# One load for 24 rows of wo, one load for wq, and multiplications of zeros ahead of the output projection

## The chip, the cores and the metric

One core of a Trainium2 chip runs the whole program. The metric is the device time of one execution in microseconds (us), smaller is better. "Span" is the time from the first to the last instruction in a profiled execution; it is about 1.9 us shorter than the device time.

The load queue is served by 16 DMA engines. A load of a 128-partition tile becomes 128 runs of contiguous bytes (packets in the trace), one for each partition, eight on each engine. PE is TensorE, DVE is VectorE, ACT is ScalarE, SP is SyncE, which issues nearly all loads here, in program order.

## The reference

A gate `g` mixes two branches of one token `x` of 1,024 numbers. Branch A is grouped attention over a cache of 65,536 positions with 4 groups of 8 query heads; branch B is a small gated feed-forward with a sequence of length 1.

```python
g = sigmoid((x * gate_w).sum(-1, keepdims=True))
q = (x @ wq)                                  # 32 heads of 128
p = softmax(einsum(q, k_cache) * 128 ** -0.5)
a = (p @ v_cache).reshape(1, 1, 4096) @ wo    # wo: 4096 x 1024, 8 MB
b = (z1 * (w_sp * layernorm(z2) + b_sp)) @ w_out
return g * a + (1 - g) * b
```

K and V are 64 MB each, wq and wo 8 MB each, and w_in and w_out 7 and 3.5 MB: 162.0 MB in all (decimal), each byte read once. The rest is small.

## The kernel before

All large loads go into one buffer `kv` of 5 slots. A slot is 32,768 bytes on each of 128 partitions (4 MB), and holds one tile of K or of V (each of the four groups has four of each). A load into a slot can be issued only when the last reader of that slot is done, and SP issues in order.

```python
kv = big.tile([P, NKV * CT * P], BF16, name="kv")          # NKV = 5 slots

def load(src, shape, at):                                   # at: slot, may be a fraction
    ...
    ins = nc.sync.dma_start(out=v, in_=src)
...
win = load(win_view, (KC, F), 3)
wq_t = [load(wq_view[:, i * KH:(i + 1) * KH, :], (KH, HD), 1 - i) for i in range(2)]
...
for g in range(1, G):
    for h in range(2):
        kn = load_kv(A_k_cache, g, 2 * h, 1 - h, 2)         # two K tiles in one load
        for i in ((0, 1), (1, 0))[h]:
            k_tile(g, 2 * h + i, kn[i])                     # DVE transposes, PE scores
        ...
        vn = load_kv(A_v_cache, g - 1, 2 * h, 3, 2)         # two V tiles in one load
        v_tile(g - 1, 2 * h, vn[0])
        if h == 1:
            stats(g)                                        # softmax of group g
        v_tile(g - 1, 2 * h + 1, vn[1])
    head_out(g - 1)                                         # this group's part of oa
for j, n, at in ((0, 2, 1), (2, 1, 3), (3, 1, 4)):          # the last group's V
    ...
keep_busy(4)
head_out(G - 1)
keep_busy(4)
```

The end of the kernel multiplies the attention output `oa` by wo, one loaded piece of rows at a time. `project` does four 128x256 matmuls for a row, on four column groups of the array. ("Row" means one of the 32 rows of wo that each partition holds, 2,048 bytes; a piece of 24 rows is one run of 49,152 bytes on every partition.) `keep_busy(n)` is n matmuls of 128x512 on a weight tile that is mostly zeros; nothing reads what they make.

```python
WO_SPLIT = ((16,), (8, 4, 2, 1, 1))
WO_BUSY = {16: 4, 8: 2, 4: 1, 2: 1, 1: 0}
for at, split in enumerate(WO_SPLIT):
    for n in split:
        t = load(wo_view[:, c0:c0 + n, :], (n, D), at + c0 % (OC // 2) * D / (CT * P))
        project(t, n, oa, c0, last=(c0 + n == OC))
        keep_busy(WO_BUSY[n])
        c0 += n
```

Of the kernel before, what the change touches and what calls it, by code (L numbers as in the profile page):

```python
# [15 lines left out]
P = 128  # L16
CT = 128
NKV = 5
B = 32
NB = P // B  # L20
VC = 4
CC = CT // VC
ZN = 448
HN = 512
WO_SPLIT = ((16,), (8, 4, 2, 1, 1))
WO_BUSY = {16: 4, 8: 2, 4: 1, 2: 1, 1: 0}


@with_exitstack
def kernel(  # L30
# [17 lines left out]
    _, _, D = A_x.shape  # L48
    _, G, S, DH = A_k_cache.shape
    HD = A_wq.shape[1]  # L50
# [4 lines left out]
    KC = D // P  # L55
    FC = FH // P
    OC = HD // P
    QD = P // H
    NT = S // (P * CT)
    HH = HN // DH  # L60
    NHB = HD // (NB * HN)
# [1 line left out]
    SCALE = float(DH) ** -0.5  # L63
    assert NB * VC * REP == P and G * B == P and B == REP * QD and DH == P and D % P == 0
    assert S % (P * CT) == 0 and F == 2 * NB * ZN and ZN == B * FC and HD == NHB * NB * HN
    assert NHB * NB == 2 * G and CC * B == 2 * HN and sum(map(sum, WO_SPLIT)) == OC

    const = ctx.enter_context(tc.tile_pool(name="const", bufs=1))
    wk = ctx.enter_context(tc.tile_pool(name="wk", bufs=2))
# [10 lines left out]
    def same_weights(ins):  # L80
        held.add(ins.ins.name)
# [91 lines left out]
    def load(src, shape, at):  # L173
        n = 1
        for s in shape:
            n *= s
        v = kv[:, int(at * CT * P):int(at * CT * P) + n]
        if len(shape) == 2:
            v = v.rearrange("p (a b) -> p a b", b=shape[1])
        ins = nc.sync.dma_start(out=v, in_=src)  # L180
        if not first_load:
            first_load.append(ins.ins.name)
        return v

    def load_kv(src, g, j, at, n=1):
        h, i = divmod(j, 2)
        rows = src[0, g, 2 * h * CT * P:2 * (h + 1) * CT * P, :].rearrange(
            "(p c) d -> p (c d)", c=2 * CT)
        v = load(rows[:, i * CT * DH:(i + n) * CT * DH], (n * CT * DH,), at)
        return [v[:, i * CT * DH:(i + 1) * CT * DH] for i in range(n)]  # L190
# [9 lines left out]
    KH = KC // 2  # L200
# [1 line left out]
    win = load(win_view, (KC, F), 3)  # L202
    win_t = [win[:, i * KH:(i + 1) * KH, :] for i in range(2)]
    wq_view = A_wq.rearrange("(p c) n -> p c n", c=KC)
    wq_t = [load(wq_view[:, i * KH:(i + 1) * KH, :], (KH, HD), 1 - i) for i in range(2)]


    row = const.tile([P, P], FP32, name="row")
# [147 lines left out]
    for k in range(NHB):  # L356
# [3 lines left out]
                                                                   j=B, e=2),  # L360
# [20 lines left out]
    def build_w(g):  # L381
        for v in range(VC):
            nc.vector.tensor_tensor(
                out=wt[g % 2][:, v, :, :, v, :],
                in0=qs[:, g].unsqueeze(2).to_broadcast([P, BP, NB, REP]),
                in1=own_n[:].unsqueeze(1).unsqueeze(3).to_broadcast([P, BP, NB, REP]),
                op=ALU.mult)

    oa = const.tile([P, OC], BF16, name="oa")
# [3 lines left out]
    def k_tile(g, j, kn):  # L393
        kb = kn.bitcast(I32)
        n = CC * DH // 2
        s_ps = pss.tile([P, 2 * HN], FP32, name="s_ps", tag="s")
        for v in range(VC):
            nc.vector.transpose(out=kb[:, v * n:(v + 1) * n], in_=kb[:, v * n:(v + 1) * n])  # L398
            while late:
                nc.vector.reduce_max(**late.pop())  # L400
            kx = kn[:, v * CC * DH:(v + 1) * CC * DH].rearrange(
                "p (c h k e) -> p h e c k", h=2, k=B, e=2)
            for b in range(BP):
                for k in range(2):
                    ins = nc.tensor.matmul(  # L405
                        s_ps[:, k * HN:(k + 1) * HN],
                        lhsT=wt[g % 2][:, v, b].rearrange("p a v h -> p (a v h)"),
                        rhs=kx[:, b // 2, b % 2, k * CC // 2:(k + 1) * CC // 2, :],
                        start=(v == 0 and b == 0), stop=(v == VC - 1 and b == BP - 1),
                        skip_group_check=True)  # L410
                    if k > 0:
                        same_weights(ins)
        if g not in mxs:
            mxs[g] = wk.tile([P, NT], FP32, name="mx")
        sct[g, j] = scp.tile([P, CC * B], BF16, name="sc")
        nc.scalar.copy(out=sct[g, j][:], in_=s_ps[:])  # L416
        late.append(dict(out=mxs[g][:, j:j + 1], in_=sct[g, j][:], axis=AX.X))
# [26 lines left out]
    def v_tile(g, j, vt):  # L444
        if j == 0:
            o_ps[g] = pso.tile([P, 2, VC * DH], FP32, name="o_ps")
        vx = vt.rearrange("p (v c d) -> p c v d", v=VC, d=DH)
        for u in range(CC // 2):
            hs = slice(u % 2 * P // 2, (u % 2 + 1) * P // 2)
            for e in range(2):  # L450
                ins = nc.tensor.matmul(  # L451
                    o_ps[g][hs, e, :],
                    lhsT=ptt[g, j][:, 2 * u:2 * u + 2, :].rearrange("p c x -> p (c x)"),
                    rhs=vx[:, 2 * u + e], start=(j == 0 and u < 2),
                    stop=(j == NT - 1 and u >= CC // 2 - 2), skip_group_check=True)
                if e > 0:
                    same_weights(ins)
# [28 lines left out]
    def keep_busy(n):  # L486
        ps = pss.tile([P, 2 * HN], FP32, name="busy_ps", tag="s")
        w = wt[G % 2][:].rearrange("p v b t u h -> p (v b t u h)")
        for i in range(n):
            ins = nc.tensor.matmul(ps[:, :HN], lhsT=w[:, :P], rhs=w[:, :HN], start=True,  # L490
                                   stop=True, skip_group_check=True)
            if i > 0:
                same_weights(ins)
# [4 lines left out]
    def project(w, n, vec, c0, first=False, last=False):  # L498
        for c in range(n):
            for t in range(NB):  # L500
                nc.tensor.matmul(  # L501
                    out_ps[t * B:(t + 1) * B, :],
                    lhsT=vec[:, c0 + c:c0 + c + 1].to_broadcast([P, B]),
                    rhs=w[:, c, t * NO:(t + 1) * NO],
                    start=(first and c == 0), stop=(last and c == n - 1),
                    skip_group_check=True)


    build_w(0)
    for j in range(NT):  # L510
        k_tile(0, j, load_kv(A_k_cache, 0, j, (2, 1, 0, 3)[j])[0])
        if j == 1:
            build_w(1)
    project(load(B_w_out.rearrange("(p c) n -> p c n", c=FC), (FC, D), 4), FC, uT, 0, first=True)
    stats(0)
    for g in range(1, G):
        for h in range(2):
            kn = load_kv(A_k_cache, g, 2 * h, 1 - h, 2)
            for i in ((0, 1), (1, 0))[h]:
                k_tile(g, 2 * h + i, kn[i])  # L520
            if h == 0 and g + 1 < G:
                build_w(g + 1)
            vn = load_kv(A_v_cache, g - 1, 2 * h, 3, 2)
            v_tile(g - 1, 2 * h, vn[0])
            if h == 1:
                stats(g)
            v_tile(g - 1, 2 * h + 1, vn[1])
        head_out(g - 1)
    for j, n, at in ((0, 2, 1), (2, 1, 3), (3, 1, 4)):
        for i, vt in enumerate(load_kv(A_v_cache, G - 1, j, at, n)):  # L530
            v_tile(G - 1, j + i, vt)
    keep_busy(4)
    head_out(G - 1)
    keep_busy(4)


    wo_view = A_wo.rearrange("(p c) n -> p c n", c=OC)
    c0 = 0
    for at, split in enumerate(WO_SPLIT):
        for n in split:  # L540
            t = load(wo_view[:, c0:c0 + n, :], (n, D), at + c0 % (OC // 2) * D / (CT * P))
            project(t, n, oa, c0, last=(c0 + n == OC))
            keep_busy(WO_BUSY[n])
            c0 += n
    out_sb = const.tile([P, NO], BF16, name="out_sb")
    out_rows = out.rearrange("o t (q n) -> (o t q) n", n=NO)
    nc.scalar.copy(out=out_sb[:], in_=out_ps[:])  # L547
# [5 lines left out]
    last = {}  # L553
# [37 lines left out]
```

## Time and profile before

| | before |
|---|---|
| device time, median | 382.93 us (3 runs), 382.97 (6 runs beside the changed kernel) |
| load queue's share of the span | 98.8% |
| PE, DVE, ACT busy | 61%, 57%, 10% |
| first load byte to last load byte | 1.0 to 378.4 us |

First the page of the kernel before: the span, the busy time of each engine, PE and DMA in 40 equal slices (tenths), the rate in GB/s per slice, the load queue (packets, MB, share of 16 engines), and the chain of waits by engine and by line.

```profile
span 381.0 us, 2602 instructions
PE 231.0 (61%) x1388; PEld 56.0 (15%) x802; DVE 218.5 (57%) x211; ACT 39.6 (10%) x55; POOL 4.4 (1%) x10
...
DMA  9999999999999999999999999999999999999995
GB/s 385 437 433 423 415 434 440 437 482 430 394 413 440 440 442 433 427 440 440 433 435 440 433 440 433 428 414 420 433 433 442 427 427 434 440 408 433 437 411 234
...
q1 hardware_dynamic: 4180, 162.01, 98.8%
...
DMA 58%; DVE 18%; PE 18%; issue 3%; ACT 2%; SPq 1%; DVEq 0%; ACTq 0%
DMA kv<-in_A_k_cache_dram 43%; PE s_ps L405 14%; DVE kv L398 12%; DMA kv<-in_A_wo_dram 9%; DMA kv<-in_A_v_cache_dram 7%; PE o_ps L451 3%; DVE pt L441 2%; DVE mx L400 2%; DVE o_sb L465 1%; ACT sc L416 1%; ACT sc L438 1%; SPq L180 1%; DVE row
```

The DMA row has no slice under 9 but the last. That is the reading on which everything rests: loads never pause. The chain of waits seems to say otherwise, with 18% each for DVE and PE. It follows one thread of who released whom, and while that thread passes through a DVE or PE instruction the DMA row still shows a full queue.

Figures come from the packet records of the trace, which no view prints. (A record has no engine's number; an engine is followed by matching the start of a packet with the end of the one before.) A run of 65,536 bytes takes one engine 2.421 us (median), which is 27.1 GB/s, or 433 for sixteen. And from first to last load, engines are without a packet for 1.9 us on average, 1.1 of them at the very end, when they finish one after another.

Second, SP's timeline of the kernel before: start, duration, engine, line, operation and what is loaded, how many. A line merges loads whose issue has only waits between.

```profile
1.66 41.59 SPq L180 DMA_DIRECT2D kv<-in_A_k_cache_dram  x4
...
95.18 0.33 SPq L180 DMA_DIRECT2D kv<-in_A_v_cache_dram  x1
118.50 0.33 SPq L180 DMA_DIRECT2D kv<-in_A_k_cache_dram  x1
...
333.56 13.33 SPq L180 DMA_DIRECT2D kv<-in_A_wo_dram  x6
```

The first wo load is issued at 333.56. By the packet records, the first engine finished the last V load ahead of it at 356.4, about 23 us later. That distance between an issue and the moment the queue would run out is the queue's lead.

Third, the end of the kernel before (timeline, weight loads left out; in brackets the idle time before and what ended it).

```profile
369.61 3.54 PE L501 MATMUL out_ps<-kv,oa 128*32 128x256 bf16 x64 [0.43 <-DVE oa L483]
373.09 1.04 PE L490 MATMUL busy_ps<-wt 128*128 128x512 bf16 x4
374.06 1.06 PE L501 MATMUL out_ps<-kv,oa 128*32 128x256 bf16 x32
...
378.96 0.29 PE L501 MATMUL out_ps<-kv,oa 128*32 128x256 bf16 x4 [0.36 <-DMA kv<-in_A_wo_dram]
379.30 0.37 ACT L547 CAST out_sb<-out_ps 128x256 bf16<-128x256 f32 x1 [44.80 <-PE out_ps L501]
```

The 64 matmuls for 16 rows take 3.54 us, 55 ns each; the 32 for the next 8 rows take 1.06, 33 ns each. The difference is PE's clock. The view by windows (us, then busy time and number for PE, weight loads, DVE, ACT, POOL, then the granted clock as a share of full speed, DMA share, GB/s) shows it:

```profile
366.10:369.50 3.40, 1.38 (x6) 0.23 (x3) 2.80 (x6) 0.00 (x0) 0.00 (x0) 1.00 0.94 400
369.50:372.90 3.40, 3.29 (x64) 2.35 (x64) 0.06 (x1) 0.00 (x0) 0.00 (x0) 0.51 0.99 417
```

PE was busy 1.38 of 3.40 us, 41%, and for the next window it got half the clock (0.51). All that costs nothing before: the last four matmuls still wait for the last row to land. (The last two columns count a run in the window in which it begins, so they jump by the length of a run; by the packet records the engines were busy all through both windows.)

### The profile page before, as it was taken

To read this page: it belongs to the slowest core of one execution; us is meant where nothing else is said; L and a number is where in the kernel's file an instruction comes from. 1 tells how busy PE (TensorE), PEld (TensorE's weight loads), DVE (VectorE), ACT (ScalarE), POOL (GpSimd) and SP (SyncE) were. 2 spreads that over 40 slices of the span, in tenths; PEclk is the share of its full clock that TensorE was granted. 3 is DMA by queue.
4 is the path that set the end of the run, shared out by engine and by line. 5 is a ranking of instruction groups with operands and counts; after the bars stand their busy time and mean duration, and the time that the engine had idled before them with its cause. 6 is when DMAs were issued, how large, how long until landed. Compare 5 with 4: busy or idle time off the path is not lost.

```text
span 381.0 us, 2602 instructions
## 1 busy us (share of the span) xinstructions
PE 231.0 (61%) x1388; PEld 56.0 (15%) x802; DVE 218.5 (57%) x211; ACT 39.6 (10%) x55; POOL 4.4 (1%) x10
## 2 busy tenths in 40 slices
PE   0064357677057934695488538872978197938376
PEld 0011011112011200121011101120111011212023
DVE  4143478996678406966976059669770398460040
ACT  1001001111601100114011001050101010410000
POOL 4000000000000000000000000000000000000000
PEclk9996659999759885999598959896789688969689
DMA  9999999999999999999999999999999999999995
GB/s 385 437 433 423 415 434 440 437 482 430 394 413 440 440 442 433 427 440 440 433 435 440 433 440 433 428 414 420 433 433 442 427 427 434 440 408 433 437 411 234
DMA packets 4231, 162.17 MB, mean 426 GB/s; under 512 B 504, under 2 KB 508, under 8 KB 892
## 3 DMA queue, kind: packets, MB, share of 16 engines
q1 hardware_dynamic: 4180, 162.01, 98.8%
q8 instruction: 8, 0.13, 0.1%
q14 instruction: 3, 0.02, 0.0%
q10 hardware_dynamic: 40, 0.01, 0.0%
HBM read 162.01 MB, written 0.00 MB: 425 GB/s over the span
## 4 chain that ended last, share of the span: by engine, by line
DMA 58%; DVE 18%; PE 18%; issue 3%; ACT 2%; SPq 1%; DVEq 0%; ACTq 0%
DMA kv<-in_A_k_cache_dram 43%; PE s_ps L405 14%; DVE kv L398 12%; DMA kv<-in_A_wo_dram 9%; DMA kv<-in_A_v_cache_dram 7%; PE o_ps L451 3%; DVE pt L441 2%; DVE mx L400 2%; DVE o_sb L465 1%; ACT sc L416 1%; ACT sc L438 1%; SPq L180 1%; DVE rowt L461 1%; PE om_ps L471 0%; DVE osum L481 0%
## 5 line engine op out<-in xcount | busy, mean ns | idle before, releaser
L405 PE MATMUL s_ps<-kv,wt 128*128 128x512 bf16 x512 | 139.7, 430 | 85.0 <-DVE kv L398 84.9
L398 DVE STREAM_TRANSPOSE kv<-kv 128x2048 int32<-128x2048 int32 x64 | 142.7, 2279 | 57.7 <-DMA kv<-in_A_k_cache_dram 57.7
L451 PE MATMUL o_ps<-kv,pt 128*64 128x512 bf16 x512 | 60.5, 394 | 7.8 <-DMA kv<-in_A_v_cache_dram 7.8
L405 PEld LDWEIGHTS <-wt 128*128 128x128 bf16 x256 | 27.2, 106 | 198.8 <-issue 138.6
L416 ACT CAST sc<-s_ps 128x1024 bf16<-128x1024 f32 x16 | 16.2, 1013 | 251.0 <-PE s_ps L405 251.0
L451 PEld LDWEIGHTS <-pt 128*64 128x64 bf16 x256 | 15.8, 114 | 49.8 <-issue 47.7
L441 DVE STREAM_TRANSPOSE pt<-sc 128x1024 bf16<-128x1024 bf16 x16 | 18.6, 1217 | 6.8 <-ACT sc L438 6.8
L400 DVE TENSOR_REDUCE mx<-sc 128x1 f32<-128x1024 bf16 x12 | 14.5, 1209 | 9.2 <-ACT sc L416 9.0
L438 ACT ACTIVATE sc<-sc,nb 128x1024 bf16<-128x1024 bf16 x16 | 18.2, 1137 | 12.2 <-DVE nb L434 12.2
L461 DVE TENSOR_TENSOR rowt<-o_ps,own 128x1024 f32<-128x1024 f32 x4 | 4.8, 1195 | 23.8 <-PE o_ps L451 23.8
L471 PE MATMUL om_ps<-o_sb,hsel 128*32 128x128 f32 x8 | 2.3, 386 | 18.7 <-DVE o_sb L465 18.7
L420 DVE TENSOR_REDUCE mx<-sc 128x1 f32<-128x1024 bf16 x4 | 4.9, 1220 | 13.6 <-ACT sc L416 13.6
L291 PE MATMUL q_ps<-kv,xT 128*32 128x512 bf16 x64 | 6.8, 604 | 4.5 <-DMA kv<-in_A_wq_dram 4.5
L247 PE MATMUL xb_ps<-xg,spread 8*128 8x256 bf16 x1 | 0.4, 365 | 13.5 <-DMA xg<-in_gate_w_dram 13.5
L465 DVE TENSOR_REDUCE o_sb<-rowt 128x128 f32<-128x1024 f32 x4 | 7.5, 1872 | 0.1
L501 PE MATMUL out_ps<-kv,oa 128*32 128x256 bf16 x128 | 6.2, 345 | 1.8 <-DMA kv<-in_A_wo_dram 1.4
L358 DVE TENSOR_TENSOR rowt<-q_ps,own_b 128x512 f32<-128x512 f32 x2 | 1.3, 687 | 9.2 <-PE q_ps L291 9.2
L291 PE MATMUL z_ps<-kv,xT 128*32 128x448 bf16 x64 | 5.4, 526 | 0.0
L251 DVE TENSOR_TENSOR xm<-xb_ps,sel_i 128x128 f32<-128x128 f32 x2 | 0.5, 286 | 8.2 <-PE xb_ps L247 8.2
L547 ACT CAST out_sb<-out_ps 128x256 bf16<-128x256 f32 x1 | 0.4, 373 | 44.8 <-PE out_ps L501 44.8
L501 PEld LDWEIGHTS <-oa 128*32 128x32 bf16 x128 | 4.0, 120 | 5.5 <-issue 3.3
L291 PEld LDWEIGHTS <-xT 128*32 128x32 bf16 x64 | 2.6, 138 | 12.6 <-issue 12.6
(90 smaller groups left out, 60.6 us busy)
## 6 DMA issues: line engine op xcount, KB each, us to landing
kv<-in_A_k_cache_dram SPq DMA_DIRECT2D x4, 4096.0 KB, 37.5
kv<-in_A_wq_dram SPq DMA_DIRECT2D x2, 4096.0 KB, 33.3
kv<-in_A_v_cache_dram SPq DMA_DIRECT2D x2, 4096.0 KB, 21.1
kv<-in_B_w_in_dram SPq DMA_DIRECT2D x1, 7168.0 KB, 19.7
kv<-in_A_wo_dram SPq DMA_DIRECT2D x1, 4096.0 KB
kv<-in_B_w_out_dram SPq DMA_DIRECT2D x1, 3584.0 KB
kv<-in_A_wo_dram SPq DMA_DIRECT2D x1, 2048.0 KB
kv<-in_A_wo_dram SPq DMA_DIRECT2D x1, 1024.0 KB, 31.3
```

What stands on the lines that cost most here:

```text
L291: ins = nc.tensor.matmul(ps[t * B:(t + 1) * B, k * HN:k * HN + n], lhsT=xT[:, i * KH + c:i * KH + c + 1].to_broadcast([P, B]), rhs=w[:, c, ...
L398: nc.vector.transpose(out=kb[:, v * n:(v + 1) * n], in_=kb[:, v * n:(v + 1) * n])
L400: nc.vector.reduce_max(**late.pop())
L405: ins = nc.tensor.matmul(s_ps[:, k * HN:(k + 1) * HN], lhsT=wt[g % 2][:, v, b].rearrange("p a v h -> p (a v h)"), rhs=kx[:, b // 2, b % 2, ...
L416: nc.scalar.copy(out=sct[g, j][:], in_=s_ps[:])
L420: nc.vector.reduce_max(**late.pop())
L438: nc.scalar.activation(out=sct[g, j][:], in_=sct[g, j][:], func=ACT.Exp, scale=SCALE, bias=nb[:, 0:1], accum_out=lss[g][:, j:j + 1])
L441: nc.vector.transpose(out=ptt[g, j][:].rearrange("p c x -> p (c x)"), in_=sct[g, j][:])
L451: ins = nc.tensor.matmul(o_ps[g][hs, e, :], lhsT=ptt[g, j][:, 2 * u:2 * u + 2, :].rearrange("p c x -> p (c x)"), rhs=vx[:, 2 * u + e], sta ...
L461: nc.vector.tensor_tensor(out=om8, in0=o_ps[g][:].rearrange("p e (v d) -> p (e v) d", d=DH), in1=own_8[:].unsqueeze(2).to_broadcast([P, 2 ...
L465: nc.vector.tensor_reduce(out=o_sb[:], in_=om8.rearrange("p x d -> p d x"), axis=AX.X, op=ALU.add)
L501: nc.tensor.matmul(out_ps[t * B:(t + 1) * B, :], lhsT=vec[:, c0 + c:c0 + c + 1].to_broadcast([P, B]), rhs=w[:, c, t * NO:(t + 1) * NO], st ...
```

## The change

Its intent: fewer and longer loads (wq in one load instead of two, 24 rows of wo in one instead of 16 + 8), which the slots have to be rotated for; and, as 24 rows now come with one landing, PE is kept multiplying zeros from the last V tile until they land, so that the 96 matmuls then run at full clock.

```diff
-WO_SPLIT = ((16,), (8, 4, 2, 1, 1))
-WO_BUSY = {16: 4, 8: 2, 4: 1, 2: 1, 1: 0}
+WO_SPLIT = (24, 4, 2, 1, 1)
+WO_BUSY = {24: 0, 4: 2, 2: 1, 1: 0}
...
-    wq_t = [load(wq_view[:, i * KH:(i + 1) * KH, :], (KH, HD), 1 - i) for i in range(2)]
+    wq = load(wq_view, (KC, HD), 0)
+    wq_t = [wq[:, i * KH:(i + 1) * KH, :] for i in range(2)]
...
-    for j in range(NT):
-        k_tile(0, j, load_kv(A_k_cache, 0, j, (2, 1, 0, 3)[j])[0])
+    for j, n, at in ((0, 1, 2), (1, 1, 3), (2, 1, 0), (3, 1, 1)):
+        for i, kn in enumerate(load_kv(A_k_cache, 0, j, at, n)):
+            k_tile(0, j + i, kn)
...
-            kn = load_kv(A_k_cache, g, 2 * h, 1 - h, 2)
-            for i in ((0, 1), (1, 0))[h]:
+            kn = load_kv(A_k_cache, g, 2 * h, 2 + h, 2)
+            for i in ((1, 0), (0, 1))[h]:
...
-            vn = load_kv(A_v_cache, g - 1, 2 * h, 3, 2)
+            vn = load_kv(A_v_cache, g - 1, 2 * h, 0, 2)
...
-    for j, n, at in ((0, 2, 1), (2, 1, 3), (3, 1, 4)):
+    for j, n, at in ((0, 2, 2), (2, 1, 1), (3, 1, 0)):
...
-    keep_busy(4)
+    keep_busy(6)
     head_out(G - 1)
-    keep_busy(4)
+    keep_busy(16)
...
-            t = load(wo_view[:, c0:c0 + n, :], (n, D), at + c0 % (OC // 2) * D / (CT * P))
+        t = load(wo_view[:, c0:c0 + n, :], (n, D), 3 + c0 * D / (CT * P))
```

More of the change, by code (lines that the diff above doesn't have):

```diff
@@ L65 @@
     assert S % (P * CT) == 0 and F == 2 * NB * ZN and ZN == B * FC and HD == NHB * NB * HN
-    assert NHB * NB == 2 * G and CC * B == 2 * HN and sum(map(sum, WO_SPLIT)) == OC
+    assert NHB * NB == 2 * G and CC * B == 2 * HN and sum(WO_SPLIT) == OC
     const = ctx.enter_context(tc.tile_pool(name="const", bufs=1))
@@ L528 @@
         head_out(g - 1)
-    for j, n, at in ((0, 2, 1), (2, 1, 3), (3, 1, 4)):
+    for j, n, at in ((0, 2, 2), (2, 1, 1), (3, 1, 0)):
         for i, vt in enumerate(load_kv(A_v_cache, G - 1, j, at, n)):
             v_tile(G - 1, j + i, vt)
-    keep_busy(4)
+    keep_busy(6)
     head_out(G - 1)
-    keep_busy(4)
+    keep_busy(16)
     wo_view = A_wo.rearrange("(p c) n -> p c n", c=OC)
     c0 = 0
-    for at, split in enumerate(WO_SPLIT):
-        for n in split:
-            t = load(wo_view[:, c0:c0 + n, :], (n, D), at + c0 % (OC // 2) * D / (CT * P))
-            project(t, n, oa, c0, last=(c0 + n == OC))
-            keep_busy(WO_BUSY[n])
-            c0 += n
+    for n in WO_SPLIT:
+        t = load(wo_view[:, c0:c0 + n, :], (n, D), 3 + c0 * D / (CT * P))
+        project(t, n, oa, c0, last=(c0 + n == OC))
+        keep_busy(WO_BUSY[n])
+        c0 += n
     out_sb = const.tile([P, NO], BF16, name="out_sb")
```

## The prediction

> **What bounds it.** The DMA stream. The page's queue table puts the load queue at 98.8% of 16 engines' span (162.01 MB, 381.0 us). In the trace's packet records the loads run from 1.0 to about 378.5 us, with engines idle under 1 us of it. A 65,536-byte run takes 2.421 us (median): 27.1 GB/s on one engine, 433 on sixteen. The Trainium skill, "DMA: Bandwidth & Descriptors", "Where 436 GB/s comes from", gives a ceiling of 435 GB/s; the trace agrees. PE (61%), DVE (57%) have slack. Two things can move the time: the queue running dry, or what follows the last landing (timeline: last projection 378.96, copy 379.30, output issued 379.69).
>
> **Removed and moved.** Same bytes.
> - wq: two loads of 32,768-byte runs (1.216 us each) become one of 65,536 (2.421): 8 x (2.432 - 2.421) = 0.09 us per engine.
> - wo: runs of 32, 16, 8, 4, 2, 2 KB take 1.216 + 0.614 + 0.313 + 0.161 + 2 x 0.085 = 2.474 us per partition. I estimate the 48 KB run, from the larger two, at 1.82, so 2.46 in all; times 8, 0.1 us. Together 0.2 us, on the bound.
> - q's matmuls begin only when all of wq is in (39.2 us in the timeline; half ran at 31.0). At the slow clock 32 took 3.2 to 3.6, so q is ready near 46 instead of 42.4, the score weights near 50.5 instead of 47. The first K tile lands at 49.85, its first transpose ends at 52.17: absorbed.
> - Slots rotate; each load waits for the mirrored tile. Queue issues (SP's timeline) should stay within a few us, except the first V pair (95.18 may become 90) and wo: its first load was issued at 333.56; now it needs the second tile of the last V pair, done near 348. The queue then still holds two V tiles, to about 359: 11 us of margin.
>
> **The end.** 24 rows land about 8 x (0.313 + 0.161 + 0.17) = 5.2 us before the last row, at 373.5. Then 96 matmuls. Before, 64 took 3.54 us at half clock, 32 took 1.06 at full. So at full clock 3.2 us, done at 376.9, and the small loads again wait only for landings: no loss. At half clock 5.3 us, done at 379: 1 to 2 us lost. The sixteen zero matmuls (0.22 to 0.43 us each) from 368.15 are to prevent that. In the clock record's windows of 3.41 us a full clock stayed where PE was busy over 50% and fell under 40%, which agrees with the Trainium skill, "TensorE: Matmul & The Clock Gate", Part 1, on idle windows. With the old phase, shares come to 53% and 60%: enough, narrowly. If the clock falls first, the zeros stretch to 373 and raise it again. PE would wait anyway.
>
> **Sum.** 382.93 - 0.2 = about 382.7 us. 80% range 382.2 to 383.5. Faster by over 2%: 0.005; within 2%: 0.985; slower: 0.01.
>
> **Right if:** load queue 98.8 to 99% of the span; span within 0.5 us of 381.0; the chain still ends in wo loads, one projection group, copy, output; the 96 matmuls take 3.0 to 3.6 us; q 3 to 4 us later with no later K landing.
>
> **Wrong if:** the 24 rows' matmuls run at half clock (up to 2 us more); the later wo issue lets the queue run dry; 48 KB rows run slower than 32 and 64 KB ones; different slots shift load rates.

## The result, and the profile after

| | before | after |
|---|---|---|
| median, 6 runs each | 382.97 us (382.82 to 383.12) | 382.78 us (382.63 to 383.09) |
| ratio of fast runs | | 0.9996, 95% interval 0.9983 to 1.0009 |
| the same, later, on another occasion (`e10_changed_again`) | 382.84 us (11 runs) | 382.60 us (5 runs); 0.9994, 0.9982 to 1.0006 |

A ratio is the mean time of one kernel's fast runs over that of the other's of the same rounds, so not quite the ratio of the medians quoted beside it. Executions over 1.5% slower than the fastest of the same kernel are left out of the means. The two differences of medians, 0.19 and 0.24 us, both agree with the predicted 0.2, but each interval holds 1, so the saving is not shown.

The page of the changed kernel, the same lines:

```profile
span 381.1 us, 2607 instructions
PE 231.3 (61%) x1397; PEld 55.6 (15%) x800; DVE 218.4 (57%) x211; ACT 39.6 (10%) x55; POOL 4.4 (1%) x10
...
DMA  9998999999999999999999999999999999999995
...
q1 hardware_dynamic: 3892, 162.01, 98.7%
...
DMA 54%; PE 23%; DVE 18%; issue 2%; ACT 2%; SPq 0%; DVEq 0%; ACTq 0%
```

The queue has 288 packets fewer (3,892 against 4,180) and carries the same 162.01 MB at practically the same share. In the packet records the mean time that an engine spends on load packets fell from 376.16 to 375.86 us, by 0.30 (in the second profile of the changed kernel to 375.94, by 0.22). There is one profile of the kernel before, and three other runs with the changed kernel's loads (`e1_no_zeros`, `e9_eight_zeros`, `e5_extra_pe`, below) gave 375.95, 375.91 and 376.14, so the fall is not much larger than the scatter. The last load byte came at 378.45 us instead of 378.42 (378.29 in the second profile). The time without a packet rose by 0.30 us in the first profile, 0.26 of it at the end: the slowest engine decides, and there the saving is of the size of the spread. In the first profile of the changed kernel the first and the last engine to finish one load are 0.9 us apart at 38 us and 2.4 us at 260.

SP's timeline of the changed kernel, lines that answer to those of before:

```profile
1.18 44.95 SPq L180 DMA_DIRECT2D kv<-in_A_k_cache_dram  x4
...
93.66 0.33 SPq L180 DMA_DIRECT2D kv<-in_A_v_cache_dram  x1
118.30 0.33 SPq L180 DMA_DIRECT2D kv<-in_A_k_cache_dram  x1
...
349.76 2.23 SPq L180 DMA_DIRECT2D kv<-in_A_wo_dram  x5
```

The steady middle is where it was (118.30 against 118.50). wo is issued at 349.76 instead of 333.56, and the stream has no hole: the last V tile was still being loaded, which kept the engines busy until 356.4 (the first) to 358.8 (the last). (The 8 in the fourth slice of the DMA row comes of counting a run in the slice where it begins; the packet records show no gap there.)

The end of the changed kernel, and its windows:

```profile
368.10 3.63 PE L491 MATMUL busy_ps<-wt 128*128 128x512 bf16 x16
...
373.92 3.24 PE L502 MATMUL out_ps<-kv,oa 128*32 128x256 bf16 x112 [2.20 <-DMA kv<-in_A_wo_dram]
...
379.00 0.29 PE L502 MATMUL out_ps<-kv,oa 128*32 128x256 bf16 x4 [0.36 <-DMA kv<-in_A_wo_dram]
379.34 0.37 ACT L548 CAST out_sb<-out_ps 128x256 bf16<-128x256 f32 x1 [44.71 <-PE out_ps L502]
```

```profile
366.10:369.50 3.40, 1.74 (x9) 0.23 (x3) 2.80 (x6) 0.00 (x0) 0.00 (x0) 1.00 1.00 434
369.50:372.90 3.40, 2.22 (x11) 0.09 (x1) 0.01 (x1) 0.00 (x0) 0.00 (x0) 1.00 0.69 292
```

The zeros run from 368.10 to 371.7. PE is busy 51% and 65% of the two windows and keeps its clock, and the matmuls for 24 rows and the next 4 (112 together) take 3.24 us, 29 ns each. They are done at 377.2, so the end is as before: four matmuls wait for the last row (0.36 us), then the copy. The copy starts at 379.34 against 379.30.

### The profile page after: what moved, and what is told of

The parts are those of the page before. It is cut to its first block, busy times and chain, and to the rows that moved or that the text cites. A ratio compares the mean times of both kernels' runs of the same rounds, so it can differ in the third digit from the quotient of the medians.

```text
span 381.1 us, 2607 instructions
## 1 busy us (share of the span) xinstructions
PE 231.3 (61%) x1397; PEld 55.6 (15%) x800; DVE 218.4 (57%) x211; ACT 39.6 (10%) x55; POOL 4.4 (1%) x10
## 3 DMA queue, kind: packets, MB, share of 16 engines
q1 hardware_dynamic: 3892, 162.01, 98.7%
HBM read 162.01 MB, written 0.00 MB: 425 GB/s over the span
## 4 chain that ended last, share of the span: by engine, by line
DMA 54%; PE 23%; DVE 18%; issue 2%; ACT 2%; SPq 0%; DVEq 0%; ACTq 0%
DMA kv<-in_A_k_cache_dram 30%; PE s_ps L406 16%; DVE kv L399 11%; DMA kv<-in_A_wq_dram 10%; DMA kv<-in_A_wo_dram 7%; DMA kv<-in_A_v_cache_dram 7%; PE o_ps L452 4%; DVE pt L442 2%; PE q_ps L292 2%; DVE mx L401 1%; DVE o_sb L466 1%; ACT sc L417 1%; ACT sc L439 1%; DVE rowt L462 1%; SPq L180 0%
## 5 line engine op out<-in xcount | busy, mean ns | idle before, releaser
L452 PE MATMUL o_ps<-kv,pt 128*64 128x512 bf16 x512 | 61.7, 400 | 6.4 <-DMA kv<-in_A_v_cache_dram 6.4
L491 PE MATMUL busy_ps<-wt 128*128 128x512 bf16 x25 | 6.1, 381 | 0.0
L502 PE MATMUL out_ps<-kv,oa 128*32 128x256 bf16 x128 | 4.2, 273 | 2.6 <-DMA kv<-in_A_wo_dram 2.6
```

What stands on the lines that cost most here:

```text
L452: ins = nc.tensor.matmul(o_ps[g][hs, e, :], lhsT=ptt[g, j][:, 2 * u:2 * u + 2, :].rearrange("p c x -> p (c x)"), rhs=vx[:, 2 * u + e], sta ...
L491: ins = nc.tensor.matmul(ps[:, :HN], lhsT=w[:, :P], rhs=w[:, :HN], start=True, stop=True, skip_group_check=True)
```

## The experiments

The theory: the time is that of an unbroken load stream; joining loads saves only what the runs themselves cost, about 0.2 us; the zeros repair a cost that the joined wo load itself brings in. All experiments are edits of the changed kernel, which stands at 382.60 to 382.78 us.

### Is the zero work needed, and for what?

`e1_no_zeros` takes the zeros away; `e2_split_no_zeros` takes them away and also loads wo's 24 rows as 16 + 8 again.

```diff
 e1 and e2:
-    keep_busy(6)
     head_out(G - 1)
-    keep_busy(16)
 e2 besides:
-WO_SPLIT = (24, 4, 2, 1, 1)
-WO_BUSY = {24: 0, 4: 2, 2: 1, 1: 0}
+WO_SPLIT = (16, 8, 4, 2, 1, 1)
+WO_BUSY = {16: 0, 8: 0, 4: 2, 2: 1, 1: 0}
```

> The changed kernel without the 6 and the 16 keep-busy matmuls around the last head's output. Theory (the zeros buy full clock for the 96 matmuls that follow the 24-row load, and that is all they do): the clock falls before 373.9 us, the 96 matmuls take 5.0 to 5.5 us instead of 3.2 and end after the last wo row has landed (378.4), so the time rises by 0.5 to 2 us against the changed kernel. Rival (the end is set by the last landing whatever the clock; the zeros are idle work): no change, within 0.2 us.

> As the run without zeros, but the 24 rows of wo as loads of 16 and 8 rows, as in the kernel before. Theory (it is the single 24-row load that makes the clock matter, since it puts 96 matmuls behind one landing 5 us before the end): the first 64 matmuls run at half clock from about 369.5 in 3.5 us, early enough, and the time is that of the changed kernel within 0.3 us. Rival (the zeros matter in any case, by the clock of the last small matmuls): as slow as the run without zeros and one load, 0.5 to 2 us over.

Measured: without zeros 384.17 us (383.49 to 384.75; ratio to before 1.0033, 1.0021 to 1.0046). Without zeros and with 16 + 8 rows 382.98 us (382.68 to 383.64; 1.0006, 0.9993 to 1.0018). The end of `e1_no_zeros` in its timeline:

```profile
373.68 5.30 PE L502 MATMUL out_ps<-kv,oa 128*32 128x256 bf16 x112 [4.52 <-DMA kv<-in_A_wo_dram]
...
380.10 0.40 PE L502 MATMUL out_ps<-kv,oa 128*32 128x256 bf16 x8
```

The same 112 matmuls take 5.30 us instead of 3.24 and end at 379.0, after the last byte of wo has come (378.20). The last matmuls no longer wait for a landing; PE does the whole tail at its own pace. With 16 + 8 rows, 64 matmuls are done before the 8 rows land, and the last four again wait for their row (two of its five runs, at 383.5 and 383.6 us, were slower than the rest, which is not explained). So the zeros are worth 1.4 to 1.6 us, and only beside the joined load: the joined load alone would have made the kernel slower by 0.3%.

`e9_eight_zeros` asks whether they must last until the landing.

```diff
-    keep_busy(16)
+    keep_busy(8)
```

> The changed kernel with 8 keep-busy matmuls after the last head's output instead of 16: they end near 370, not 371.7. Theory (what counts is that PE is over half busy in every window up to the landing of the 24 rows at 373.9): the clock falls in the window before the landing, the 96 matmuls take about 5.3 us, and the time is 0.5 to 2 us over the changed kernel. Rival (some zeros are enough, since they only have to end the idle time before the output): no change, within 0.2 us.

Measured: 383.69 us (383.32 to 385.22; 1.0031, 1.0017 to 1.0045), 1.1 us over the changed kernel on the same chip. Its windows (the profiled run is its slowest, 385.22 us):

```profile
369.50:372.90 3.40, 0.59 (x3) 0.09 (x1) 0.10 (x1) 0.00 (x0) 0.00 (x0) 1.00 0.68 289
372.90:376.40 3.50, 2.51 (x49) 2.15 (x52) 0.00 (x0) 0.00 (x0) 0.00 (x0) 0.51 0.97 384
```

With PE busy for 17% of the window before the landing, the clock is halved (0.51) just as the 24 rows arrive. How long the zeros last matters, not that there are some.

### What does a load cost when the queue is full?

`e4_short_rows` takes the opposite of joining to its end; `e7_wq_halves` undoes the joining of wq alone.

```diff
 e4:
-WO_SPLIT = (24, 4, 2, 1, 1)
+WO_SPLIT = (1,) * 24 + (4, 2, 1, 1)
 e7:
-    wq = load(wq_view, (KC, HD), 0)
-    wq_t = [wq[:, i * KH:(i + 1) * KH, :] for i in range(2)]
+    wq_t = [load(wq_view[:, i * KH:(i + 1) * KH, :], (KH, HD), i) for i in range(2)]
```

> The changed kernel with the 24 rows as 24 loads of one row (2,048-byte runs) instead of one of 49,152-byte runs. Theory (with the queue full, a load costs only what its runs cost on the engines): 24 x 8 x 0.085 = 16.3 us instead of 14.6, so the time rises by 1.5 to 2.2 us. Rival (each load pays a fixed cost of its own[...], and joining loads is worth that): a rise of 10 to 46 us.

> The changed kernel with wq as two loads again. Theory (joining the two saves about 0.1 us of stream): the time is the same within 0.3 us, the load queue's busy time rises by about 0.1 us, and q is ready near 42.5 us instead of 45.8 without moving any later load's landing. Rival (an earlier q lets K tiles and so later loads go earlier): more than 0.5 us faster.

Measured: 24 loads instead of one, 384.91 us (384.49 to 385.26; 1.0052, 1.0038 to 1.0066), so 2.1 to 2.3 us more than the changed kernel, at or just over the top of the range expected. Runs of 2,048 bytes took 88 ns on average. The 24 rows took an engine 16.85 us (18.23 for all such runs, less 1.38 for the last two rows), where its runs of 49,152 bytes took 14.56 (eight of 1.820): 2.3 us more. The last load byte came 1.5 us later than in the first profile of the changed kernel, and PE, at half clock from 377.3 in that profile, added the rest. That is 0.1 us for each of the 23 loads more, where the rival's 10 to 46 us would be 0.4 to 2. wq in halves: 382.80 us (382.66 to 382.95; 0.9999), no difference; the mean engine time on loads was 375.95, within the scatter of the two profiles of the changed kernel (375.86 and 375.94), so the 0.1 us of that part is below what these runs resolve.

### Is the late issue of wo free, and what if the queue runs dry?

`e3_wo_late` puts wo into the slots of the last V tiles, so its first load must wait longer.

```diff
-        t = load(wo_view[:, c0:c0 + n, :], (n, D), 3 + c0 * D / (CT * P))
+        t = load(wo_view[:, c0:c0 + n, :], (n, D), c0 * D / (CT * P))
```

> The changed kernel with wo's rows put into slots 0 and 1 instead of 3 and 4, so that the first wo load must wait for the last V tile (done near 364.5 us) instead of the second of the last four (near 349). Theory (only an unbroken stream matters; the later issue of the change was free because two V tiles were still queued): the queue runs dry near 358.5 and restarts about 1 us after the issue; the time rises by 6 to 7.5 us. Rival (wo's issue has slack, since PE is not ready for it before 369): the rise is under 2 us.

Measured: 392.89 us (392.45 to 392.98; 1.0257, 1.0241 to 1.0272), 10.1 to 10.3 us more than the changed kernel and more than I had expected. SP's timeline, and PE's for the first rows of wo:

```profile
365.01 2.35 SPq L180 DMA_DIRECT2D kv<-in_A_wo_dram  x5
...
381.97 5.80 PE L502 MATMUL out_ps<-kv,oa 128*32 128x256 bf16 x112 [9.80 <-DMA kv<-in_A_wo_dram]
```

The engines finished the last V load between 356.26 and 358.87, not all at 358.5, and the first byte of wo came at 365.96, 0.95 us after the start of the issue. (The issue takes 0.33 us, so that is 0.62 after its end; the Trainium skill, "DMA: Bandwidth & Descriptors", "Latency and other measured facts", gives about 0.6 us to the first byte of a load that SP issues, without saying from where it counts.) That left an engine idle for 8.7 us on average. Runs just after the restart were slow (those of 49,152 bytes 1.901 us on average against 1.820, over eight of them 0.65 us). But the engines now finished within 0.4 us of each other instead of 2.4, so the 24 rows were at work 8.0 us later than in the changed kernel (381.97 against 373.92). The zeros had ended at 372.2, the clock fell to half at 377.0, and the 112 matmuls took 5.80 us instead of 3.24, 2.6 more. These 10.6 us, less the 0.6 that the changed kernel spends waiting for the last rows, are the 10.0 by which the last copy starts later (389.35 against 379.34). The last byte of wo, at 387.97, did not set the end: the last eight matmuls began at 388.90. (It was late on one engine only, beside an instruction transfer of 16,384 bytes from 385.70; the others were done at 386.6.) So the theory's mechanism stands, and my size was short: I had left out the spread of the engines, the slow restart and the clock.

### Does compute hold any of the time?

`e5_extra_pe` adds PE work, after each K tile.

```diff
         nc.scalar.copy(out=sct[g, j][:], in_=s_ps[:])
+        keep_busy(8)
         late.append(...)
```

> The changed kernel with 8 more unused matmuls of 128x512 after every one of the 16 K tiles: 128 matmuls, about 28 us more PE work at full clock. Theory (the DMA stream bounds it and the 23% of PE and 18% of DVE in the chain of waits are work hidden beside a stream that never stops): the time stays within 0.5 us. Rival (what the chain of waits names is on the path): up to 28 us more, at least 5.

Measured: 382.89 us (382.7 to 383.88; 0.9999, 0.9984 to 1.0015). Recorded PE busy time rose from 231.3 to 250.0 us, less than the added work (128 of about 0.22 us); that fits the higher mean clock (0.861 against 0.839), but was not taken apart. So PE could be given more work at no cost: its share in the chain of waits was not on the path. (The profiled run was the slowest of the four, 383.88 us.) No run adds work to DVE, the other engine in that chain.

`e6_fewer_bytes` takes 3.67 MB of loads away: the product with w_out reads the K tile in slot 3 instead. Its output is wrong, which doesn't matter for the time.

```diff
-    project(load(B_w_out.rearrange(...), (FC, D), 4), FC, uT, 0, first=True)
+    project(kv[:, 3 * CT * P:3 * CT * P + FC * D].rearrange("p (a b) -> p a b", b=D), FC, uT, 0, first=True)
```

> The changed kernel without the load of w_out (3.67 MB of 162.0 MB); the product reads another tile instead, so the result is wrong on purpose. All compute stays. Theory (time is bytes over the stream's rate of 162.0 MB in 377.4 us): the time falls by 8.0 to 9.0 us. Rival (compute shares the path, 46% of the chain by engine is not DMA): it falls by 5 us or less.

Measured: 395.4 us (394.31 to 395.73; 1.0323), 12.6 to 12.8 us slower with fewer bytes. The experiment was badly built, and instructive. Its page and SP's timeline:

```profile
DMA  9999999703799999999999999999999999999995
GB/s 373 480 426 403 441 430 426 326 0 102 333 459 459 459 426 421 426 426 426 426 433 428 426 426 433 453 454 447 426 426 421 426 426 434 426 418 436 444 409 240
```

```profile
97.05 0.33 SPq L180 DMA_DIRECT2D kv<-in_A_k_cache_dram  x1
```

Slot 3 is where the next K pair goes. In the changed kernel that load needs only the first two K tiles to be done and is issued at 71.95; now it must also wait for the product, which PE does after all four K tiles. It was issued at 97.05, and the queue stood dry from about 78 to 98 us. The engine time on loads fell by 8.0 us (367.86 from 375.86), as the theory has it, and the time without a packet rose by 20.8 (22.94 from 2.17): 12.8 us more in sum, which is what was measured. So it says nothing against the theory, but it doesn't test what it was built to test.

Three more runs take bytes away without a new wait: some V pairs are loaded narrower, and the second tile's matmuls read from the middle of what came. The results are those of other data, though all three passed the comparison's tolerance.

```diff
-            vn = load_kv(A_v_cache, g - 1, 2 * h, 0, 2)
+            if <e8: h == 0 and g >= 2;  e11: g >= 2;  e12: h == 0>:
+                v = load(rows[:, :w], (w,), 0)      # w: e8 1.5 tiles; e11 and e12 1.75
+                vn = [v[:, :CT * DH], v[:, w - CT * DH:]]
+            else:
+                vn = load_kv(A_v_cache, g - 1, 2 * h, 0, 2)
```

> The first try at fewer bytes also made a K load wait for the product and broke the stream. Here two of the V pairs (groups 1 and 2, first halves) are loaded one and a half tiles wide instead of two, 4.19 MB less in all, and the second tile's matmuls read from the middle of what was loaded: same instructions of compute, same waits, a wrong result on purpose. Theory (time is bytes over the stream's rate, 433 GB/s): 9.2 to 10.0 us faster than the changed kernel, stream idle still near 2 us. Rival (compute in the chain of waits, 46% of it, holds part of the time): less than 5 us faster.

> The same 4.19 MB less as in the run before, but taken in four places (each V pair of groups 1 and 2 is loaded 1.75 tiles wide instead of 2), so that the queue's lead shrinks by 2.4 us at a time instead of 4.85; a wrong result on purpose. In the run before, 4.85 us was more than the lead allowed: the queue ran dry for 1.7 us near 196 us and the runs after the restart were slower, and 6.3 of the 9.7 us came through. Theory (bytes over rate, as long as the queue never runs dry): 9.0 to 10.0 us faster than the changed kernel, no idle stretch inside the stream. Rival (the rest of the 9.7 us is held by compute, not by the dry queue): again 6 to 7 us.

> 3.15 MB less: only the V pair between a group's two K pairs is cut, by a quarter tile, in all three groups; a wrong result on purpose. In the two runs before, a K load was issued as late as 271.8 us, when the queue had just run out, since VectorE was still busy with the group's turn when that group's first K pair landed (257 us landed, 260 begun). In the place cut here the queue's lead in the changed kernel is 4.7 to 5.7 us for the engine that is first done, and the cut takes 2.4 of it. Theory (bytes over rate as long as no queue runs dry; the lead, not mean busy share, is the slack): 6.6 to 7.5 us faster than the changed kernel, no dry stretch. Rival (compute holds back part of any saving of bytes, about a third): 4 to 5 us.

| run | MB less | at 433 GB/s | time | faster than 382.60 by | ratio to before |
|---|---|---|---|---|---|
| `e8_bytes_cut` | 4.19 | 9.7 us | 376.27 us (375.66 to 377.13) | 6.3 us | 0.9823 (0.9808 to 0.9837) |
| `e11_quarter_cut` | 4.19 | 9.7 us | 376.82 us (375.93 to 377.70) | 5.8 us | 0.9849 (0.9826 to 0.9873) |
| `e12_first_halves` | 3.15 | 7.3 us | 376.11 us (375.47 to 377.06) | 6.5 us | 0.9823 (0.9802 to 0.9844) |

The first two fell short of the theory's ranges. The last, on its medians, came just short of its range (6.6 to 7.5), and far over its rival's 4 to 5. In the packet records of the profiled run of each (the slowest of four, the fastest of four at 375.93 us, and the second slowest at 376.68), idle engine time was 4.8 us in the first (1.7 of it a hole near 196 us), 3.2 in the second (0.5 of it a hole near 272 us), and 2.2 with no hole in the last (the changed kernel: 1.9 and 2.2). Where the second one's hole comes from is seen in DVE's timeline at the turn of a group, next to the same place of the changed kernel:

```profile
259.63 0.29 DVE L484 TENSOR_SCALAR oa<-osum,rl,gw 32x32 bf16<-32x32 f32 x1
259.95 11.08 DVE L399 STREAM_TRANSPOSE kv<-kv 128x2048 int32<-128x2048 int32 x5
```

```profile
262.52 0.29 DVE L484 TENSOR_SCALAR oa<-osum,rl,gw 32x32 bf16<-32x32 f32 x1
262.84 11.08 DVE L399 STREAM_TRANSPOSE kv<-kv 128x2048 int32<-128x2048 int32 x5
```

SP's next K load, in the same order:

```profile
271.77 0.33 SPq L180 DMA_DIRECT2D kv<-in_A_k_cache_dram  x1
```

```profile
274.85 0.33 SPq L180 DMA_DIRECT2D kv<-in_A_k_cache_dram  x1
```

In both, DVE goes straight from the last step of the old group's output to the transposes of the new group's first K pair. In the changed kernel that pair was reported as landed at 262.45, 0.4 us earlier; in `e11_quarter_cut` at 257.56, 2.4 us earlier. So of a landing 4.9 us earlier only 2.9 us became earlier work. The next K load (which needs the first K tile done) was issued 3.1 us earlier (271.77 against 274.85), but the first engine ran out of queued work 7.1 us earlier (271.8 against 278.9): a lead of 4.0 us had shrunk to nothing. Mean busy shares of 57 and 61% don't show that; the lead at each issue does.

Even so, holes account for only 1.7 and 0.5 us. (The expectation for the last run puts the leads at 4.7 to 5.7 us; for group 3's pair it was these 4.0.) In all three runs, runs of 65,536 bytes took longer (2.435 to 2.441 us on average against 2.425), 0.9 to 1.3 us in all, in spells, mostly on several engines at once; and in the first two, engines lost 0.6 to 1.0 us more at the end, where they finish one after another. Why runs are slower in such spells where the queue has little lead but no hole is recorded is open, and with it why none of the three reached bytes over rate.

`e10_changed_again` is the changed kernel itself, beside `e8_bytes_cut` and `e9_eight_zeros`; its numbers stand in the table of the result.

> The changed kernel itself, unedited, on the same chip as the two others, for a direct comparison and a tighter ratio to the kernel before. Theory: 382.6 to 383.1 us, within 0.1% of the kernel before; the saving of 0.2 us from longer runs is below what the spread of the engines' last landings (0.8 to 2.4 us between the first and the last engine) lets show.

No version that loads every byte beat both kernels by more than the noise. At 433 GB/s in the largest runs, of the 435 that the Trainium skill, "DMA: Bandwidth & Descriptors", "Where 436 GB/s comes from", gives as the ceiling, there is little left between the first and the last byte, and the 1.0 us before and the 2.6 us after are the same in both.

## Why the prediction was right

- **What bounds it.** Right. The load stream is unbroken in both; 128 more matmuls cost nothing (`e5_extra_pe`), and a hole of 8.7 us cost 10 (`e3_wo_late`). "Engines idle under 1 us" holds up to the end only: 1.9 us with the 1.1 at the end. The phrase "PE, DVE have slack" was too simple: at the turn of a group DVE is busy until within 1 us of when the next K pair lands, and the slack there is the queue's lead.
- **What joining saves.** Right in size: 0.2 us were predicted, engine time fell by 0.30 and 0.22, the medians by 0.19 and 0.24. From the median time of single runs it is 8 x (2 x 1.216 - 2.421) + 8 x (1.216 + 0.614 - 1.819) = 0.18 us: each run that is saved saves about 0.011 us. That the last landing moves by as much is not shown; the spread between engines is larger. The estimate of 1.82 us for a run of 49,152 bytes met 1.819 (median).
- **q later, absorbed.** Right: q's matmuls ended at 45.75 instead of 42.4, the first K transpose began at 50.24 instead of 49.85, and no load landed later for it. (It now waits for DVE to build the score weights, until 50.3, and no longer for the K tile, reported as landed at 49.62.)
- **wo's late issue.** Right that the queue holds out, with less margin: 348 predicted, 349.76 found, and the queue would not have run out before 356.4 on the first engine and 358.8 on the last. The margin was 6.6 to 9.1 us rather than 11: the issue came 1.8 us later than estimated, and the spread of the engines was left out. "The queue then still holds two V tiles" was wrong: one, begun, was left.
- **The end.** Right: 24 rows predicted to land at 373.5 and found at work from 373.92; PE busy shares of 53 and 60% predicted, 51 and 65% found, and the clock held. The 96 matmuls took 2.80 us (112 took 3.24), less than the 3.2 predicted and the 3.0 to 3.6 of its conditions; it decides nothing, as PE waits for the last rows anyway. What would follow at half clock, "1 to 2 us lost", was tested: 1.4 to 1.6 us without zeros.
- **The sum.** 382.7 predicted, 382.78 and 382.60 measured. The closeness is partly luck: 0.2 us is within the scatter, and a forecast of no change at all would have fitted as well. What the experiments show is the mechanism, not the 0.2. (One more condition, a load queue of 98.8 to 99% of the span, was met in the second profile and missed by 0.1 in the first.)

## What to carry to other kernels

Where the load queue is full from the first byte to the last, joining loads is worth only what the shorter runs cost extra on the engines (here 0.2 us of 383 by the packet records), and work on other engines is free up to the queue's lead (shown for added PE work; for DVE, seen where the lead was used up), which has to be read at each issue and not from mean busy shares. A larger last load brings a larger block of matmuls behind one landing near the end, so it needs PE's clock at that moment; zeros can hold it if they fill enough of the clock's window before the landing (65% did, 17% did not), but here 16 + 8 rows made the clock irrelevant and gave the same time within the noise. To test a bound by taking bytes away, check first that no load has to wait for something new.

## What the Trainium skill lacked or had wrong

- "DMA: Bandwidth & Descriptors", "Rules for kernel authors", advises large transfers, and the page ("Anatomy of one DMA — SWDGE (gpsimd) path") gives a fixed 2 us for one DMA, measured on the path of GpSimd and mostly the wait for completion. It has no figure for what one more load costs in a full queue: 24 loads of 256 KB instead of one of 6 MB cost 2.1 to 2.3 us in all, 0.1 us a load; one run of 2,048, 32,768, 49,152, 65,536 bytes took 0.085, 1.216, 1.819, 2.421 us (medians).
- The same page, "Where 436 GB/s comes from", has a ceiling that fits (435 GB/s; the largest runs made 433), but its remark that for transfers between HBM and SBUF the HBM side (about 358) binds did not hold for this one core: 162.0 MB came in 377.4 us, 429 GB/s.
- No page says how far the engines drift apart in a long stream: 0.9 us between first and last at 38 us, 2.4 us at 260, in steps; in the three profiles of the two kernels, after the first 5 us, every run that was over 0.1 us slow (0.37 to 0.66 us over) begins as an instruction transfer ends, most of these of 16,384 bytes, which took an engine about 1.0 to 1.1 us. That they cause the steps is inferred from the times.
- "TensorE: Matmul & The Clock Gate", Part 1, speaks of idle windows. Here a window with PE busy for 41% (and one with 17%) was already followed by half clock, while 51% and 65% kept it. Over all 14 traces, in the clock record's own steps of 3.41 us at full clock: after all 183 with PE busy under 38% the clock was halved, after all 754 over 43% it stayed, and between them 8 of 27 kept it. So 51% was less narrow than the prediction thought.
- Nothing on the restart of a dry queue beyond the first byte: after 8.7 us of idleness the runs of the first load took 4% longer (1.901 against 1.820 us on average). The first loads after the holes of `e6_fewer_bytes` and `e8_bytes_cut` took an engine 20.06 us for eight runs of 65,536 bytes, 3.5% over the usual 19.38.
